# One product for the sums of keys and queries, k'v turned in one product, whole levels for two batches, and a new order of all operations

## The chip, the cores and the metric

The kernel runs on one core of a Trainium2 chip. The core has TensorE (PE: matmuls and weight loads), VectorE (DVE), ScalarE (ACT), GpSimd (POOL), SyncE (SP, which issues most transfers) and 16 DMA engines. The metric is the device time of one execution in microseconds, as the median of several runs. Times within the kernel come from one profiled execution.

## The reference, cut to what matters

The first part is a polynomial sketch attention over 4 batches, 4 heads, 1088 positions and head size 32. The second part mixes tokens with two 1088 x 1088 matrices.

```python
def phi(x):                                   # r = 8, so 64 features
    a = np.einsum('rd,bhsd->bhsr', S1, x)
    b = np.einsum('rd,bhsd->bhsr', S2, x)
    return np.einsum('bhsi,bhsj->bhsij', a, b).reshape(*x.shape[:-1], r * r)
q_p, k_p = phi(q), phi(k)
kv = np.einsum('bhsf,bhsd->bhfd', k_p, v)
z = np.sum(k_p, axis=2)
x = (q_p @ kv) / (q_p @ z + 1e-6)             # heads joined: (4, 1088, 128)
theta = x @ w_theta
zr, zi = x * np.cos(theta), x * np.sin(theta)
y = einsum('ts,bsd->btd', w_tok_r, zr) + einsum('ts,bsd->btd', w_tok_i, zi)
u = x + y
out = u + np.maximum(u @ w_ch, 0.0)
```

S1, S2 and the weights of the second part are 64-bit floats, which the kernel reads as pairs of 32-bit words and converts itself.

## The kernel before, in words

The tokens of a batch are 9 chunks of 128 (the last half empty), taken in 3 groups of 3 chunks. Heads and head size make the 128 columns.

A batch goes through these stages. `kfeatures` (741 to 774) transposes the keys, makes their features, forms outer products on DVE (761) and sums k'v on PE (770) in 32 columns of the array per head; ACT copies the sum to `kvT` (774). `key_sums` rounds the keys to a grid and forms their Gram matrix: the sum of squares of the keys comes from ACT (644 or 650), is added over the partitions by a product with ones (653) and gives the four steps `kg` (655); the Gram products (690, 703, 704 or 693) are in two halves of 64 columns; ACT copies parts of them (708, 709 or 698) for two turned products (712 or 701). `query_scale` does the same sum for the queries (937, 940) and derives their scale. `chain` (795 to 882) turns the Gram matrix into the denominators' vector for batch 0, for batch 1, and for batches 2 and 3 together: e0 and e1 on DVE and ACT (795 to 798), a first product (809), a second (847), a maximum (852), and slices `mv`, `mf`. `chain_out` turns k'v with two products, one for each half of the output's rows (901), and multiplies it by a mask (902). `query_slices` transposes and splits the queries (969 to 980). `levels` (1001) multiplies the queries by the slices, 9 products in f16 and 3 in f32 for a group, each in two halves of 64 columns of the array. DVE forms the denominators (1009 to 1030). `outputs_x` forms the outer products of the queries (1052), transposes them (on PE for batches 0 and 1, on DVE and over DRAM for 2 and 3), multiplies by k'v (1077), and then takes angle, sine and cosine (1105 to 1130).

The 17 rows of the mixing matrices are read and converted by `weight` (583 to 590): one transfer of 1.1 MB, two ACT passes, two DVE passes. `mix_row` uses a row for batch 0 in three spans of 384, 384 and 320 tokens, and for batch 1 span by span. Batches 2 and 3 share seven products in the manner of Winograd (1266), in pieces of 288 and 256 or 128 tokens. `finish` and `finish_turned` make the output.

All operations are entered by `op` with an engine and a duration. They aren't issued as they are entered: the string `ORDER` gives the numbers of all 1022 operations in the order of issue, each engine's queue being a subsequence, and `PLACES` gives the slot of each buffer in its class (8 banks of PSUM, 5 slots for raw rows, 22 large ones, and so on). An engine takes its operations strictly in that order. `SPINS` puts products on zeros (line 379, tile `idle`) ahead of certain operations of PE, which keep it busy: 10 at the start, 16 by the string, and one in the code.

Most of PE's products are issued from line 341, most of DVE's operations from lines 305, 309 and 312, so they are told apart by tile.

Of the kernel before, what the change touches and what calls it, by code (L numbers as in the profile page):

```python
# [21 lines left out]
P = 128  # L22
# [44 lines left out]
)  # L67
PLACES = (
# [8 lines left out]
)  # L77
SPINS = (
    "70:2 15:3 137:1 211:1 424:2 128:1 168:1 174:2 176:1 521:2 "
# [14 lines left out]
QGRAM = (False,) * 4  # L94
# [7 lines left out]
ADD_FLY2 = 3.1  # L102
QFIX = 2.006
# [18 lines left out]
class Layout:  # L122
# [63 lines left out]
    def issue(self, pools, fill):  # L186

        spins = dict(tuple(map(int, x.split(":"))) for x in SPINS.split())
        shared = True
        for o in self.order:  # L190
            n, home = spins.get(o.i, 0), None
            if shared:
                for _ in range(n):
                    fill()
            for b in o.bufs:
                if b.ap is None:
                    raw = pools[b.cls](b.slot)
                    home = raw if b.cls == "ps" else home
                    b.ap = view(raw, b.shape, b.dt)
            if not shared:  # L200
                for _ in range(n):
                    fill(home)
            o.fn()
            shared = shared and o is not self.parted
# [33 lines left out]
def kernel(  # L238
# [136 lines left out]
    idle = fixed((GW,), BF16, "idle")  # L375
    nowhere = buf("ps", (GW,), F32, "nowhere")

    def spin(home=None):
        T.matmul(nowhere() if home is None else view(home, (GW,), F32), idle()[:, 0:P], idle(), start=True, stop=True, skip_group_check=True)  # L379

    op("G", 0.3, lambda: G.memset(idle(), 0.0), [idle], [])  # L381
    op("P", 1.73, lambda: [spin() for _ in range(10)], [nowhere], [idle])
# [235 lines left out]
    kvb, kk, kg = {}, {}, {}  # L618

    def key_sums(b):  # L620
        at("grid", b)
        kx = ld["k", b]
        km = buf("sm", (3,), F32, "km")
        kb = buf("hf", (NC, HD), BF16, "kb")
# [7 lines left out]
        if ("k", b) in SPLIT:  # L632
# [8 lines left out]
            op("V", 0.2, lambda: V.tensor_reduce(out=km()[:, 1:2], in_=ka(), axis=AX.X, op=ALU.add), [(km, 1)], [ka])  # L641
        elif KHALF[b]:
            c = (NC + 1) // 2 * HD
            op("A", act(c) + 0.1, lambda: A.activation(flat(j_())[:, :c], kc()[:, :c], AF.Square, accum_out=km()[:, 1:2]),
               [(j_, 0), (km, 1)], [kx])
# [767 lines left out]
```

## Time and profile before

| | |
|---|---|
| median of 3 runs | 219.61 us (219.26 to 220.01) |
| span of the profiled execution, first to last instruction | 217.4 us |
| median less that span | 2.2 us |
| PE busy | 209.3 us, 1998 matmuls |
| DVE busy | 181.2 us |
| ACT busy | 111.2 us |
| POOL busy | 22.2 us |
| moved by DMA | 40.58 MB |
| mean granted clock of PE | 0.997 |

The profiled execution has no time of its own beside its span, so the span is set against the median of the runs. In a row of the timeline the first number is the start in us, the second the length; `ps<-big,zs 128*128 128x384 f32 x6` is six matmuls from tiles big and zs into PSUM, with weights of 128 rows and 128 columns and 384 streamed columns. An f32 product is two such instructions, so a mixing row of batch 0 is six. `128*64`, `128*32` and `64*64` are weights that fill a part of the array. A length includes the drain of a matmul, so neighbours overlap by some 0.15 us.

### The profile page before, as it was taken

Reading aid. Unit: us, or ns where it says so; the run is one execution under the profiler, and the core shown is the slowest. Engines: PE = TensorE matmul, PEld = TensorE weight load, DVE = VectorE, ACT = ScalarE, POOL = GpSimd, SP = SyncE. Lnnn points to the kernel's source line nnn. Section 1 sums busy time; section 2 is a strip of 40 time slices with the busy share of each in tenths; the row PEclk is TensorE's granted clock in tenths of the full one; section 3 lists DMA queues with packets and bytes.
Section 4 is the critical chain, followed back from the end, with each engine's and each line's share of the span. In section 5 each row is a group of like instructions: output and inputs, shape, how many; then the busy total and the mean of one; then the engine's idle time right before and its main releaser. Section 6 shows DMA issues by size and latency. Waiting matters only on the chain.

```text
span 217.4 us, 5063 instructions
## 1 busy us (share of the span) xinstructions
PE 209.3 (96%) x1998; PEld 154.3 (71%) x1998; DVE 181.2 (83%) x408; ACT 111.2 (51%) x214; POOL 22.2 (10%) x44
## 2 busy tenths in 40 slices
PE   7999899999999999999999999999999999999994
PEld 3987786686766686666766575667758788888883
DVE  4899999999999999999599839988138999996542
ACT  3998498899779999983322040354037400000010
POOL 2237000055000000100132000100101000000000
PEclk9999999999999999999999999999999999999998
DMA  5999996869979979894226998599911000045253
GB/s 153 429 406 340 425 399 203 333 224 271 267 276 361 361 264 380 219 198 126 33 36 102 222 137 199 105 156 151 231 78 32 0 0 0 3 66 89 36 79 75
DMA packets 52635, 40.58 MB, mean 187 GB/s; under 512 B 45444, under 2 KB 47108, under 8 KB 50436
## 3 DMA queue, kind: packets, MB, share of 16 engines
q1 hardware_dynamic: 35540, 33.71, 48.7%
q0 software_dynamic: 1728, 4.65, 10.5%
q10 hardware_dynamic: 15344, 1.90, 6.0%
q8 instruction: 15, 0.25, 0.5%
q14 instruction: 8, 0.07, 0.1%
HBM read 30.43 MB, written 5.18 MB: 164 GB/s over the span
## 4 chain that ended last, share of the span: by engine, by line
PE 72%; DVE 12%; ACT 8%; DMA 4%; ACTq 2%; issue 2%; SPq 1%
PE ps L341 66%; DMA big<-q_l 2%; DVE lv L305 2%; PE ps L1064 2%; ACTq L333 2%; PE ps L1098 1%; DMA fx<-g 1%; DVE g L305 1%; DVE big L305 1%; PE ps L967 1%; ACT big L584 1%; ACT big L937 1%; DVE hf L309 1%; DVE zs L305 1%; ACT g L1068 1%
## 5 line engine op out<-in xcount | busy, mean ns | idle before, releaser
L341 PE MATMUL ps<-big,zs 128*128 128x384 f32 (+4 forms) x398 | 109.7, 424 | 0.4 <-DVE zs L305 0.4
L341 PEld LDWEIGHTS ps<-big,zs 128*128 128x128 f32 x398 | 71.4, 190 | 30.3 <-issue 2.6
L1201 ACT COPY g<-ps 128x128 f32<-128x128 f32 (+1 forms) x3 | 0.9, 301 | 42.5 <-PE ps L1193 42.5
L305 DVE CUSTOM_DVE_ANT_0 big<-big,big 128x2176 uint16<-128x2176 uint16 x17 | 21.8, 1287 | 0.4 <-ACT big L586 0.2
L584 ACT ACTIVATE big<-zs 128x1088 f32<-128x1088 f32 x17 | 20.9, 1235 | 2.1 <-DMA zs<-w_tok 1.2
L586 ACT ACTIVATE big<-zs 128x1088 int32<-128x1088 uint32 (+1 forms) x18 | 21.3, 1184 | 0.1
L341 PE MATMUL ps<-big,big 128*64 128x64 f32 (+2 forms) x208 | 20.6, 276 | 0.0
L341 PEld LDWEIGHTS ps<-big,big 128*64 128x64 f32 (+1 forms) x208 | 16.5, 154 | 2.9 <-issue 0.2
L305 DVE TENSOR_TENSOR big<-big,big 128x544 f32<-128x544 f32 x24 | 16.7, 712 | 0.0
L1002 ACT COPY lv<-ps 128x480 f32<-128x480 f32 x12 | 6.3, 563 | 14.2 <-PE ps L341 14.2
L312 DVE SCALAR_TENSOR_TENSOR g<-g,ps 128x384 f32<-128x384 f32 x12 | 6.6, 548 | 8.1 <-ACT g L1111 8.1
L1078 ACT COPY big<-ps 128x384 f32<-128x384 f32 x12 | 5.9, 489 | 14.0 <-PE ps L341 8.3
L309 DVE TENSOR_SCALAR big<-big 128x1088 int32<-128x1088 int32 x17 | 12.2, 724 | 0.6 <-ACT big L584 0.5
L341 PEld LDWEIGHTS ps<-w,big 128*128 128x128 f32 x80 | 10.6, 192 | 2.3 <-ACT g L1068 0.6
L319 POOL DMA_DIRECT2D big<-hf x6 | 5.4, 957 | 63.3 <-DVE g L312 33.8
L319 POOL DMA_DIRECT2D g<-big x6 | 5.2, 920 | 64.8 <-ACT g L1179 34.7
L341 PE MATMUL ps<-w,big 128*128 128x128 f32 x80 | 11.8, 280 | 0.0
L305 DVE TENSOR_TENSOR g<-lv 128x768 f32<-128x768 f32 x12 | 11.2, 945 | 0.0
L341 PE MATMUL ps<-g,sm 128*64 128x384 f32 x48 | 10.1, 507 | 0.2 <-ACT big L1078 0.2
L305 DVE TENSOR_TENSOR zs<-ps,g 128x768 f32<-128x768 f32 (+2 forms) x15 | 9.4, 632 | 1.0 <-PE ps L1098 0.9
L341 PEld LDWEIGHTS <-hf 128*64 128x64 f16 (+1 forms) x288 | 7.7, 110 | 2.9 <-issue 1.7
L379 PE MATMUL ps<-idle 128*128 128x384 bf16 x27 | 7.8, 400 | 1.3 <-POOL idle L381 1.3
(194 smaller groups left out, 336.6 us busy)
## 6 DMA issues: line engine op xcount, KB each, us to landing
zs<-w_tok SPq DMA_DIRECT2D x17, 1088.0 KB, 7.0
big<-k_l SPq DMA_DIRECT2D x6, 576.0 KB, 6.6
big<-hf POOLq DMA_DIRECT2D x6, 576.0 KB, 6.0
big<-v_l SPq DMA_DIRECT2D x4, 576.0 KB, 7.0
g<-fq SPq DMA_DIRECT2D x6, 384.0 KB, 5.2
big<-q_l SPq DMA_DIRECT2D x3, 576.0 KB, 5.1
fq<-g SPq DMA_DIRECT2D x12, 96.0 KB, 4.0
fq<-g ACTq DMA_DIRECT2D x12, 96.0 KB, 4.1
```

What stands on the lines that cost most here:

```text
L305: eng.tensor_tensor(out=o, in0=a, in1=b, op=f)
L309: (eng or V).tensor_scalar(out=o, in0=a, scalar1=s1, scalar2=s2, op0=op0, **kw)
L312: (eng or V).scalar_tensor_tensor(out=o, in0=a, scalar=s, in1=b, op0=op0, op1=op1)
L319: op("G", 0.9, lambda: G.dma_start(dst(), src(), accum_op=ALU.add), w, r, fly=fly)
L333: E.dma_start(there().rearrange("(a i) (x b j) -> b i x a j", a=nf, b=nf, j=SQ)[f], blocks()[f * SQ:(f + 1) * SQ].rearrange("i (x a j) -> ...
L341: T.matmul(o, lhs, rhs, start=start, stop=stop, skip_group_check=True)
L379: T.matmul(nowhere() if home is None else view(home, (GW,), F32), idle()[:, 0:P], idle(), start=True, stop=True, skip_group_check=True)
L584: op("A", 0.22 + n * 0.0009, lambda: A.activation(dfn(), words_of(raw(), n)[1].bitcast(F32), AF.Prelu, scale=2.0**-112, alpha=-(2.0**32)), ...
L586: op("A", 0.22 + n * 0.0009, lambda: A.activation(stp(), words_of(raw(), n)[0].bitcast(U32), AF.Copy, scale=2.0**-29), [stp], [raw])
L1002: op("A", act(480), lambda g=g, lp=lp: A.copy(lv().rearrange("p l (c n) -> p l c n", n=HR)[:, :, g * GC:(g + 1) * GC], lp().rearrange("p c ...
L1064: T.transpose(tr()[:, i * P:(i + 1) * P], qp()[:, i * H + 2 * n:i * H + 2 * n + 2].rearrange("p h i j -> p (h i j)"), ident())
L1078: op("A", act(GW), lambda g=g, xp=xp: A.copy(xt()[:, g * GW:(g + 1) * GW], xp()), cells(xt, g * GW, (g + 1) * GW), [xp])
```

## The change

Sums: `key_sums` no longer has a product with ones. The sums of squares of a chain's keys and of its first query stand side by side in one buffer `kq`, and `query_scale` of the chain's first batch adds them in one product; the steps `kg` of those keys come from it. Four of eight such products go, and `kg` depends on a query's square. `query_scale` of batches 2 and 3 follows both `key_sums`.

k'v: ACT writes the copy twice side by side, and one product with 128 weight columns turns it.

Levels: for batches 0 and 1 (`LFULL`) a product has all 128 weight columns, 12 products a group in place of 24, and f32 products stand between the f16 ones, chunk by chunk.

Zeros: `idle` is f32; four 16-bit products on zeros become one f32 product of the same 384 columns. `SPINS` has 5 in place of 16.

`finish_turned` also takes widths that are multiples of 64. The unused branch `QGRAM` goes. `ORDER` and `PLACES` are new throughout, for 1018 operations.

```diff
 SPINS = (
-    "70:2 15:3 137:1 211:1 424:2 128:1 168:1 174:2 176:1 521:2 "
+    "76:2 166:2 172:1 "
 )
+LFULL = (True, True, False, False)
...
-    idle = fixed((GW,), BF16, "idle")
+    idle = fixed((GW,), F32, "idle")
...
-    op("P", 1.73, lambda: [spin() for _ in range(10)], [nowhere], [idle])
+    op("P", 1.73, lambda: [spin(None, n) for n in (4, 4, 2)], [nowhere], [idle])
...
-        kg[b] = fixed((4,), F32, f"kg{b}")
-        pg = buf("ps", (512,), F32, "pg")
-        op("P", 0.25, lambda: mm(pg()[:, 0:1], ones(), km()[:, 1:2], True, True), [pg], [(km, 1)])
-
-        vop(4, lambda: tt(V, kg[b](), steps(), pg()[:, 0:1].to_broadcast([P, 4]), ALU.mult), [kg[b]], [pg, steps])
...
-        kt = buf("sm", (R * R,), F32, "kvT")
-        op("A", act(R * R), lambda: A.copy(kt(), acc()), [kt], [acc])
+        kt = buf("sm", (2, R * R), F32, "kvT")
+        op("A", act(2 * R * R), lambda: A.copy(kt(), bc(acc(), 1, [P, 2, R * R])), [kt], [acc])
...
-            def twice(tr=tr, kt=kt):
-                for n in range(2):
-                    mm(tr()[n * R * R:(n + 1) * R * R], kt(), ident(), True, True)
-
-            op("P", 0.31, twice, [tr], [kt, mk], half=True)
+            op("P", 0.23, lambda tr=tr, kt=kt: mm(tr(), kt().rearrange("p n f -> p (n f)"), ident(), True, True), [tr], [kt, mk])
...
-        t = buf("ps", (1,), F32, "qt")
-        op("P", 0.25, lambda: mm(t(), ones(), m()[:, 0:1], True, True), [t], [m])
+        t = buf("ps", (1 + len(keys_of),), F32, "qt")
+        op("P", 0.25, lambda: mm(t(), ones(), kq(), True, True), [t], [kq])
+        for j, kb_ in enumerate(keys_of):
+            kg[kb_] = fixed((4,), F32, f"kg{kb_}")
+            col = j + (j > 0)
+            vop(4, lambda kb_=kb_, col=col: tt(V, kg[kb_](), steps(), t()[:, col:col + 1].to_broadcast([P, 4]), ALU.mult),
+                [kg[kb_]], [t, steps])
...
-            def lev(g=g, lp=lp):
+            parts = [slice(0, P)] if LFULL[b] else sides
+
+            def lev(g=g, lp=lp, sides=parts):
...
-                for i in range(GC):
                     x = f()[:, (g * GC + i) * P:(g * GC + i + 1) * P]
                     for n in sides:
-                        mm(o[n, i, 2 * HR:], x[:, n], mf[b]().rearrange("p t h r -> p (t h r)"), False, True)
-
-            op("P", 0.91, lev, [lp], [f, h, mv[b], mf[b]], half=True)
+                        mm(o[n, i, 2 * HR:], x[:, n], mf[b]().rearrange("p t h r -> p (t h r)"), False, i == GC - 1)
+
+            op("P", 1.03 if LFULL[b] else 0.91, lev, [lp], [f, h, mv[b], mf[b]], half=not LFULL[b])
...
-        n = w // P
+        n = -(-w // P)
+        m = w // n
...
-                end = finish_turned if h and not (c1 - c0) % P else finish
+                end = finish_turned if h and not (c1 - c0) % (P // 2) else finish
...
             kfeatures(b)
             key_sums(b)
+        for b in bs:
             query_scale(b)
```

Of the new order, what the prediction speaks of: SP loads query 1 ahead of query 0, w2 ahead of keys 3, values 0 and keys 2, and row 5 behind row 0. On ACT one conversion of row 0 stands ahead of batch 1's Gram copies (708, 709) and one more of row 4 ahead of chain 1's step at 798. On PE the k'v sums of batch 0 stand ahead of chain 0's second product, operations on parts of the array stand together more often, and mixing rows 6 to 11 of batch 0 come ahead of chain 2's first product. On DVE rows 5 to 11 are finished ahead of batch 1's last outer products.

More of the change, by code (lines that the diff above doesn't have):

```diff
@@ L93 @@
 KTWO = (False, False, True, True)
-QGRAM = (False,) * 4
 QDMA = (False, False, True, True)
@@ L191, in issue @@
             n, home = spins.get(o.i, 0), None
+            sizes = [4] * (n // 4) + [1] * (n % 4)
             if shared:
-                for _ in range(n):
-                    fill()
+                for x in sizes:
+                    fill(None, x)
             for b in o.bufs:
@@ L200, in issue @@
             if not shared:
-                for _ in range(n):
-                    fill(home)
+                for x in sizes:
+                    fill(home, x)
             o.fn()
@@ L373, in constants, with spin @@
         V.memset(ones(), 1.0)
-    idle = fixed((GW,), BF16, "idle")
+    idle = fixed((GW,), F32, "idle")
     nowhere = buf("ps", (GW,), F32, "nowhere")
-    def spin(home=None):
-        T.matmul(nowhere() if home is None else view(home, (GW,), F32), idle()[:, 0:P], idle(), start=True, stop=True, skip_group_check=True)
+    def spin(home=None, quarters=1):
+        o = nowhere() if home is None else view(home, (GW,), F32)
+        x = idle() if quarters > 1 else idle().bitcast(BF16)
+        w = GW * quarters // 4 if quarters > 1 else GW
+        T.matmul(o[:, :w], x[:, 0:P], x[:, :w], start=True, stop=True, skip_group_check=True)
     op("G", 0.3, lambda: G.memset(idle(), 0.0), [idle], [])
-    op("P", 1.73, lambda: [spin() for _ in range(10)], [nowhere], [idle])
+    op("P", 1.73, lambda: [spin(None, n) for n in (4, 4, 2)], [nowhere], [idle])
     op("V", 1.55, constants, [hm, bdm, halfpi, ups, steps, upv, ones], [])
@@ L615, in load @@
                                                         src[b].rearrange("p c h d -> p (c h d)")), [t], [])
-    kvb, kk, kg = {}, {}, {}
+    kvb, kk, kg, both, bothp = {}, {}, {}, {}, {}
     def key_sums(b):
@@ L623, in key_sums @@
         km = buf("sm", (3,), F32, "km")
+        first = next(bs[0] for bs in CHAINS if b in bs)
+        if b == first:
+            both[b] = buf("sm", (1 + sum(len(bs) for bs in CHAINS if b in bs),), F32, "kq")
+        kq, kc_ = both[first], (b - first) + (b > first)
         kb = buf("hf", (NC, HD), BF16, "kb")
@@ L640, in key_sums @@
                 op("A", act(n / NG) + 0.1, lambda g=g: square(g), [(j_, g), (ka, g)], [(kx, g)])
-            op("V", 0.2, lambda: V.tensor_reduce(out=km()[:, 1:2], in_=ka(), axis=AX.X, op=ALU.add), [(km, 1)], [ka])
+            op("V", 0.2, lambda: V.tensor_reduce(out=kq()[:, kc_:kc_ + 1], in_=ka(), axis=AX.X, op=ALU.add), [(kq, kc_)], [ka])
         elif KHALF[b]:
             c = (NC + 1) // 2 * HD
-            op("A", act(c) + 0.1, lambda: A.activation(flat(j_())[:, :c], kc()[:, :c], AF.Square, accum_out=km()[:, 1:2]),
-               [(j_, 0), (km, 1)], [kx])
+            op("A", act(c) + 0.1, lambda: A.activation(flat(j_())[:, :c], kc()[:, :c], AF.Square, accum_out=kq()[:, kc_:kc_ + 1]),
+               [(j_, 0), (kq, kc_)], [kx])
             op("V", dve(n - c) + 0.06, lambda: V.tensor_tensor_reduce(
                 flat(j_())[:, c:], kc()[:, c:], kc()[:, c:], 1.0, 0.0, ALU.mult, ALU.add, km()[:, 2:3]), [(j_, 1), (km, 2)], [kx], lk=1)
-            op("V", 0.16, lambda: tt(V, km()[:, 1:2], km()[:, 1:2], km()[:, 2:3], ALU.add), [(km, 1)], [(km, 2)], lk=1)
-        else:
-            op("A", act(n) + 0.1, lambda: A.activation(flat(j_()), kc(), AF.Square, accum_out=km()[:, 1:2]), [j_, (km, 1)], [kx])
-        kg[b] = fixed((4,), F32, f"kg{b}")
-        pg = buf("ps", (512,), F32, "pg")
-        op("P", 0.25, lambda: mm(pg()[:, 0:1], ones(), km()[:, 1:2], True, True), [pg], [(km, 1)])
-        vop(4, lambda: tt(V, kg[b](), steps(), pg()[:, 0:1].to_broadcast([P, 4]), ALU.mult), [kg[b]], [pg, steps])
+            op("V", 0.16, lambda: tt(V, kq()[:, kc_:kc_ + 1], kq()[:, kc_:kc_ + 1], km()[:, 2:3], ALU.add),
+               [(kq, kc_)], [(km, 2)], lk=1)
+        else:
+            op("A", act(n) + 0.1, lambda: A.activation(flat(j_()), kc(), AF.Square, accum_out=kq()[:, kc_:kc_ + 1]), [j_, (kq, kc_)], [kx])
         def key_step():
             x = km()[:, 0:1]
-            ts(x.bitcast(I32), km()[:, 1:2].bitcast(I32), 1, ALU.logical_shift_right)
+            ts(x.bitcast(I32), kq()[:, kc_:kc_ + 1].bitcast(I32), 1, ALU.logical_shift_right)
             ts(x, x, 2.0**76, ALU.mult)
-        op("V", 0.36, key_step, [(km, 0)], [(km, 1)], lk=1)
+        op("V", 0.36, key_step, [(km, 0)], [(kq, kc_)], lk=1)
         at("keys", b)
@@ L908 @@
     even = fixed((6,), F32, "even")
-    if any(QGRAM):
-        idh = fixed((HW,), F32, "idh")
-        at("tiny")
-        small(lambda: tt(G, idh(), ident()[:, 0:HW], ident()[:, HW:HD], ALU.add), [idh], [])
     def cells(x, t0, t1):
@@ L919, in query_scale @@
         x = ld["q", b]
-        m = buf("sm", (3,), F32, "qm")
+        m = buf("sm", (1,), F32, "qm")
+        mine = [bs for bs in CHAINS if bs[0] == b]
+        keys_of = list(mine[0]) if mine else []
+        kq = both[b] if mine else buf("sm", (1,), F32, "kq")
+        c = min(1, len(keys_of))
         n = NC * HD
         f = qx[b] = buf("big", (n,), F32, "qx")
-        if QGRAM[b]:
-            pq = buf("ps", (HW,), F32, "pq")
-            dg = buf("sm", (HW,), F32, "qd")
-            def gram():
-                for c in range(NC):
-                    y = x()[:, c].rearrange("p h d -> p (h d)")
-                    for n in sides:
-                        mm(pq()[n], y[:, n], y[:, n], c == 0, c == NC - 1)
-            op("P", 1.05, gram, [pq], [x], half=True)
-            op("V", 0.3, lambda: V.tensor_tensor_reduce(dg(), pq(), idh(), 1.0, 0.0, ALU.mult, ALU.add, m()[:, 0:1]),
-               [dg, m], [pq, idh])
-        else:
-            op("A", act(n) + 0.1, lambda: A.activation(f(), x().rearrange("p c h d -> p (c h d)"), AF.Square,
-                                                       accum_out=m()[:, 0:1]), [f, m], [x])
-        t = buf("ps", (1,), F32, "qt")
-        op("P", 0.25, lambda: mm(t(), ones(), m()[:, 0:1], True, True), [t], [m])
+        op("A", act(n) + 0.1, lambda: A.activation(f(), x().rearrange("p c h d -> p (c h d)"), AF.Square,
+                                                   accum_out=kq()[:, c:c + 1]), [f, (kq, c)], [x])
+        t = buf("ps", (1 + len(keys_of),), F32, "qt")
[5 more added lines that the diff above has]
+                [kg[kb_]], [t, steps])
         s = qs[b] = fixed((2,), F32, f"qs{b}")
         def scale():
-            a = m()[:, 1:2]
-            ts(a, t(), QFIX, ALU.mult, TINY, ALU.max)
+            a = m()
+            ts(a, t()[:, c:c + 1], QFIX, ALU.mult, TINY, ALU.max)
             ai = a.bitcast(I32)
@@ L950, in query_scale @@
         op("V", 0.53, scale, [m], [t])
-        op("A", 0.2, lambda: A.mul(s()[:, 0:1], m()[:, 1:2], 2.0**-49), [(s, 0)], [m])
+        op("A", 0.2, lambda: A.mul(s()[:, 0:1], m(), 2.0**-49), [(s, 0)], [m])
         small(lambda: ts(s()[:, 1:2], s()[:, 0:1], s()[:, 0:1], ALU.mult, ec()[:, 1:2], ALU.mult, eng=G), [(s, 1)],
@@ L1192, in turn @@
             for c in range(n):
-                T.transpose(ut()[:, c], u()[:, c * P:(c + 1) * P], ident())
+                T.transpose(ut()[:m, c], u()[:, c * m:(c + 1) * m], ident())
         def times():
             for c in range(n):
-                mm(po()[:, c], u()[:, c * P:(c + 1) * P], w2()[:, 1], True, True)
+                mm(po()[:m, c], u()[:, c * m:(c + 1) * m], w2()[:, 1], True, True)
         op("P", 0.11 * n, turn, [ut], keys)
         op("P", 0.22 * n, times, [po], keys + [w2])
-        op("A", act(w), lambda: A.copy(ot(), ut()), [ot], [ut])
-        vop(w, lambda: stt(ot(), po(), 0.0, ot(), ALU.max, ALU.add), [ot], [po])
-        op("S", 0.0, lambda: SY.dma_start(out[b, t0:t0 + w].rearrange("(c j) d -> j c d", j=P), ot()), [], [ot],
+        op("A", act(n * P), lambda: A.copy(ot()[:m], ut()[:m]), [ot], [ut])
+        vop(n * P, lambda: stt(ot()[:m], po()[:m], 0.0, ot()[:m], ALU.max, ALU.add), [ot], [po])
+        op("S", 0.0, lambda: SY.dma_start(out[b, t0:t0 + w].rearrange("(c j) d -> j c d", j=m), ot()[:m]), [], [ot],
            lk=1, fly=1.8, n=w)
```

88 rows, old and new, of tables (ORDER, PLACES) are left out of this document.

## The prediction

> **What bounds the kernel now.** I read the page first: the engines' shares, then the slices, then the chain that ended last.
>
> ```profile
> span 217.4 us, 5063 instructions
> PE 209.3 (96%) x1998; PEld 154.3 (71%) x1998; DVE 181.2 (83%) x408; ACT 111.2 (51%) x214; POOL 22.2 (10%) x44
> ...
> PE   7999899999999999999999999999999999999994
> ...
> DVE  4899999999999999999599839988138999996542
> ...
> PEclk9999999999999999999999999999999999999998
> DMA  5999996869979979894226998599911000045253
> GB/s 153 429 406 340 425 399 203 333 224 271 267 276 361 361 264 380 219 198 126 33 36 102 222 137 199 105 156 151 231 78 32 0 0 0 3 66 89 36 79 75
> ...
> PE 72%; DVE 12%; ACT 8%; DMA 4%; ACTq 2%; issue 2%; SPq 1%
> ```
>
> A slice is 5.4 us. PE is busy in nearly all of them at full granted clock, and 72% of the chain is PE's. But a busy PE includes matmuls on zeros (line 379), and DVE shows a 9 in slices 3 to 19, to about 103 us, as well. So two engines are full at once for the first half, and the chain in order of time is needed to tell them apart, with the sums by stretch:
>
> ```profile
> 61.04 0.88 DVE g L305
> ...
> 83.10 44.99 PE ps L341 x362
> ```
>
> ```profile
> 20.00:35.00 15.00, 13.27 (x332) 11.05 (x332) 14.79 (x40) 10.55 (x24) 0.29 (x2) 1.00 0.97 388
> ...
> 50.00:62.00 12.00, 11.82 (x107) 8.13 (x107) 11.82 (x27) 10.02 (x17) 2.09 (x3) 1.00 0.97 263
> 102.00:128.00 26.00, 26.00 (x297) 17.75 (x296) 18.95 (x36) 6.68 (x12) 4.25 (x6) 1.00 0.58 112
> ```
>
> (Columns: stretch, length, busy PE, weight loads, DVE, ACT, POOL, clock, DMA share, GB/s.) From 20 to 35 us DVE is full (14.79 of 15.00) and PE is not. From 50 to 62 us both are, and the outer products of batch 1 (the DVE piece at 61.04) stand in the chain. In 102 to 128 us DVE has 7 us to spare and PE none. I therefore sum in three parts: to 35 us by DVE, ACT and loads, 35 to 62 us by DVE or PE, whichever gains less, and after 62 us by PE.
>
> **Prices on PE.** These rows are the timeline of PE; differences of starts are used, because the length of a row includes the drain of its last matmul.
>
> ```profile
> 57.31 2.10 PE L341 MATMUL ps<-big,zs 128*128 128x384 f32 x6
> 59.34 0.34 PE L341 MATMUL ps<-ident,g 64*64 64x64 f32 x4
> ...
> 70.57 1.99 PE L341 MATMUL ps<-big,zs 128*128 128x384 f32 x6
> 72.40 0.49 PE L1098 MATMUL ps<-ident,big 128*128 128x128 f32 x3
> ```
>
> One mixing row between whole-array neighbours takes 72.40 - 70.57 = 1.83 us, and the same six matmuls between neighbours that use parts of the array (64*64, 128*64, 128*32) take 59.34 - 57.31 = 2.03 us. So a change of partition on both sides costs the neighbour 0.20 us.
>
> ```profile
> 102.10 0.57 PE L341 MATMUL ps<-mv,hf 128*64 128x96 f16 x18
> ...
> 103.02 0.55 PE L341 MATMUL ps<-mv,hf 128*64 128x96 f16 x18
> 103.40 0.68 PE L341 MATMUL ps<-mf,big 128*64 128x96 f32 x12
> 103.91 0.55 PE L341 MATMUL ps<-mv,hf 128*64 128x96 f16 x18
> ...
> 104.90 6.40 PE L341 MATMUL ps<-big,zs 128*128 128x320 f32 x20
> ```
>
> A group of levels in halves takes 103.91 - 103.02 = 0.89 us, and the last group before whole-array work takes 0.99 us, 0.10 more. A stretch of partitioned work therefore costs 0.20 + 0.10 = 0.30 us beyond its matmuls.
>
> ```profile
> 74.98 0.54 PE L341 MATMUL ps<-g,big 128*32 128x64 f32 x24
> 75.46 0.66 PE L341 MATMUL ps<-sbt,sm 64*64 64x64 f32 x16
> 76.04 0.88 PE L341 MATMUL ps<-g,big 128*32 128x64 f32 x48
> 76.85 0.94 PE L341 MATMUL ps<-w,big 128*128 128x128 f32 x6
> ```
>
> 24 matmuls of 128*32 take 0.48 us with a start and 48 take 0.81 us, so 24 alone cost 0.33 and a change of shape inside a stretch up to 0.15 us; I take 0.1, and 0 to 0.15 as bounds.
>
> **The new order.** I read off both orders by name. Operations on part of the array are the key features (64 columns), Gram products, halves of levels and numerators, k'v sums (32 columns) and the small 64*64 turns. Before, from chain 1's first product (34.9 us) to batch 1's first transposes there are 6 such stretches with 6 inner changes of shape, afterwards 3 with 5. From there to the end there were 9 with 7, and are 7 with 3. Levels of batch 1 and three turns of k'v that are now whole are counted in that. The saving is 3 x 0.30 + 1 x 0.1 = 1.0 us to 62 us, and 2 x 0.30 + 4 x 0.1 = 1.0 us after it. At 0.20 a stretch and nothing inside the two would be 0.6 and 0.4.
>
> **Levels over all columns.** Nothing in the trace has 128 weight columns in f16. The halves stream 9 f16 pairs in 103.40 - 103.02 = 0.38 us and 6 f32 pairs in 0.51 us, and streams of a whole product are no longer than those of its pair. The weight load is the question.
>
> ```profile
> 88.42 0.78 PE L341 MATMUL ps<-sm,pbd 128*128 128x128 f32 x6
> 89.03 2.05 PE L341 MATMUL ps<-big,zs 128*128 128x384 f32 x6
> ...
> 55.85 0.45 PE L341 MATMUL ps<-hf 128*64 128x64 bf16 x18
> 56.13 1.25 PE L341 MATMUL ps<-big,big 128*64 128x64 f32 x36
> ```
>
> Six f32 products with whole weights, four of them only 64 wide, take 0.61 us: 0.10 each, though streaming 64 is half of streaming 128. So f32 weights cost about 0.10 us each. In 16 bit, 18 loads of 64 columns take 0.28 us, or 0.031 per pair. Bounds for a group: 0.89 us if every load hides, 15 x 0.102 = 1.53 us if 16-bit weights cost what f32 ones do. I take 0.38 + 6 x 0.105 = 1.01, and 0.04 for the more frequent turns from f16 to f32, 1.05 us, since the 16-bit row is the nearer. That is +0.16 a group, +0.5 us for batch 1 (0 to +1.9). Batch 0's groups run at 25 to 28 us under DVE's full queue, at no cost; uncovered they add the same 0.5.
>
> The Trainium skill ("TensorE: Matmul & The Clock Gate", LDWEIGHTS (loading the stationary operand)) states that a load takes its columns divided by 1.2 in ns, whatever the contraction. For 128 columns that is 107 ns, which agrees with the 0.10 us of the f32 row; for 16 bit it would be 53 ns per 64 columns, and the trace, at 31 ns per pair, disagrees. By the page a group would be an estimated 15 x 0.107 = 1.6 us.
>
> **Turns and ones-products.**
>
> ```profile
> 55.58 0.44 PE L341 MATMUL ps<-ident,sm 128*64 128x128 f32 x4
> ...
> 90.92 0.28 PE L341 MATMUL ps<-sm,ones 128*128 128x8 f32 x2
> ```
>
> A turn of k'v in two halves takes 55.85 - 55.58 = 0.27 us; whole it is two loads, 0.21 us, so 0.06 less, 3 x after 62 us: 0.15. The doubled copy on ACT is 64 elements longer, behind which nothing waits soon: 0. Of the ones-products (0.28 us with the drain) four go, all before 35 us, where PE isn't the bound: 0. The key's step kg now also waits for the first query's square, on DVE with chain 0's e0 right behind it. But e0 also needs the turned Gram sums, whose ACT copy comes four ACT operations behind the query's square, so kg isn't last: 0, and up to 0.5 if the square is.
>
> **Zeros.** The group of zero products, and a piece of the chain:
>
> ```profile
> L379 PE MATMUL ps<-idle 128*128 128x384 bf16 x27 | 7.8, 400 | 1.3 <-POOL idle L381 1.3
> ...
> 38.51 0.33 PE ps L379 x2
> ```
>
> Of the 27 the work of 11 goes, 0.33 / 2 = 0.16 us each. After 35 us five were there and one is left: 0.65 us; the two at 38.51 stand where chain 1 is waited for, so I take 0.3 (0 to 0.65). The f32 zeros at the start stream as long in fewer instructions, and POOL's zeroing of twice the bytes is covered by the first keys' load. The other rule for turned stores changes nothing: 288 is no multiple of 64, and 256 and 128 were turned already.
>
> **To 35 us.** Here the order decides. In SP's queue query 1 is moved ahead of query 0, the weights w2 ahead of keys 3, values 0 and keys 2, and row 5 behind row 0. In ACT's queue, half of row 0's conversion now stands ahead of batch 1's Gram copy (line 708), and half of row 4's ahead of chain 1's e0 (798).
>
> ```profile
> L584 ACT ACTIVATE big<-zs 128x1088 f32<-128x1088 f32 x17 | 20.9, 1235 | 2.1 <-DMA zs<-w_tok 1.2
> ...
> 27.24 1.48 ACT L1002 COPY lv<-ps 128x480 f32<-128x480 f32 x3 [2.57 <-PE ps L341]
> ...
> 31.38 0.29 ACT L708 COPY g<-ps 128x128 f32<-128x128 f32 x1
> ...
> 34.54 0.35 ACT L798 ACTIVATE sm<-sm,kg 128x64 f32<-128x64 f32 x1 [0.91 <-DVE sm L312]
> ...
> 24.70 0.80 SPq L583 DMA_DIRECT2D zs<-w_tok  x2
> ```
>
> ACT idled 2.57 + 0.91 us there, room for the two conversions (1.235 us each). Row 0 is issued at 24.70 and its bytes come at the 400 GB/s of slices 2 to 6: with row 5 (1.1 MB) behind it and keys 3's second copy (0.6 MB) ahead, it lands 0.5 / 0.4 = 1.3 us earlier than before. The Gram copy then comes at about its 31.4 us. Chain 1 starts as before: 0. The bounds are a gain of 1.0 (DVE has a denominator step of batch 0 less ahead of e0) and a loss of 1.5 (a landing as late as if row 5 were still ahead). PE's k'v sums of batch 0 move ahead of chain 0's second product, so values 0 must have landed by then: they are the eighth load instead of the seventh, 0.26 MB or 0.6 us later, and needed earlier; I take 0 and leave it to the rival below.
>
> **The sum.** 35 to 62 us: PE gains 1.0 + 0.3 - 0.5 = 0.8; DVE has kg2, batch 1's k'v multiply and two of chain 2's e steps less ahead of batch 1's first outer product.
>
> ```profile
> 33.64 0.28 DVE L312 SCALAR_TENSOR_TENSOR sm<-ps,kg,g 128x64 f32<-128x64 f32 x1
> ```
>
> Four like this step are 1.1 us at most; the next begins before the last one's end, so I take 0.7. The lesser of the two counts, 0.7. After 62 us: 1.0 + 0.15 = 1.15. Together 1.85 us. The span would be 215.5 and, with the 2.2 us by which the median 219.61 exceeds it, the time **217.8 us**. The end of the order is as before, so its 3.4 us behind PE stays.
>
> **Rivals.**
> Row 0 comes late (the other side). Its load waits for a free buffer (SP's 24.70 follows a pause), and the buffers are assigned anew. ACT stands in order, so the Gram copy, chain 1 and all of PE's static order move with it, us for us. It must land by 30.2 (31.4 less a conversion); from 2.5 us beyond, 32.7, the kernel is slower by 0.66; one more 1.1 MB row ahead is 2.8 us and gives 220.6. For it: a DMA share of 0.97 there; against it: fewer bytes ahead. 0.27, in which I put any other in-order stall of this kind.
> 16-bit weights cost as much as f32 ones: batch 1's groups add 1.9 instead of 0.5, 219.2 us, no change. The 31 ns speaks against it. 0.05. (The Trainium skill's rule of columns over 1.2, as above, would give about the same.)
> Loads eat half: row 0 is late by 1.5 us, 219.3. 0.05.
> The forecast and what lies about it, 215.6 to 218.9: 0.63. Nearer its own bounds: 216.4 to 218.9.
>
> **The numbers.** About 0.3% (0.66 us) is what a measurement of this kernel can tell from no change. Faster 0.63, within it 0.10, slower 0.27. The range goes from all gains at their bounds without DVE's limit (to 35 us 1.0; to 62 us 0.9 + 0.15 + 0.65; after it 0.6 + 0.6 + 0.15: 4.0 less, 215.6) to the first rival with half a row more (221.0).
>
> **What would show it.** Right: the number of whole-array rows with 2.03 us falls, a level group of batch 1 takes 1.0 to 1.1 us, chain 1's first product (64*64) starts at 34 to 35.5 us, batch 3's levels end 1.5 us earlier than 128. Wrong: ACT idle on a load of w_tok before the Gram copy, a first product of chain 1 after 37 us, level groups of 1.5 us, or new PE waits for DVE between 62 and 128 us, because the mixing rows 6 to 11 are taken earlier.

## The result and the profile after

The changed kernel takes 217.0 us (median of 11 runs, 216.66 to 219.75) against 219.86 us for the kernel before beside it (11 runs, 219.26 to 221.81). The ratio is 0.988 with a 95% interval of 0.985 to 0.991, a gain of 2.6 us. Here and below, medians and ratios leave out runs more than 1.5% above the fastest of their kernel, and a ratio can differ a little from the quotient of two medians. The profiled execution took 216.8 us with a span of 215.0 us. The forecast was 217.8 us, in a range of 215.6 to 221.0.

In the changed kernel line numbers shift a little: most products are issued from line 340, zeros from 381, most DVE work from 304, 308 and 311. The page, in the same parts as before:

```profile
span 215.0 us, 4841 instructions
PE 205.4 (96%) x1877; PEld 154.8 (72%) x1877; DVE 182.6 (85%) x408; ACT 110.9 (52%) x214; POOL 22.9 (11%) x44
...
PE   7989899999999999999999999899999999999993
...
DVE  4899999999999999989899589778849999994631
...
PEclk9999999999999999999999999999999999999999
DMA  5999999999896997007633988889954201103143
...
PE 77%; DVE 11%; DMA 5%; ACT 3%; issue 2%; ACTq 0%; POOL 0%; SPq 0%; DVEq 0%; POOLq 0%
```

PE still bounds it, with 3.9 us less work and the clock at full. The PE row has a new dent in slice 26, at 134 to 140 us. Transfers are fuller up to some 64 us. The timeline of PE shows the dent (a wait for a transfer at 135.27 us) and the marks by which the forecast is judged:

```profile
23.17 0.25 PE L340 MATMUL ps<-hf 128*64 128x64 bf16 x4 [0.91 <-issue]
...
34.36 0.61 PE L340 MATMUL ps<-sbt,sm 64*64 64x64 f32 x8
...
61.09 0.82 PE L1053 MATMUL ps<-ident,g 128*128 128x128 f32 x6
...
123.38 0.32 PE L340 MATMUL ps<-mv,hf 128*64 128x96 f16 x6
...
135.27 1.51 PE L340 MATMUL ps<-g,sm 128*64 128x384 f32 x8 [1.39 <-DMA g<-fq]
...
156.20 2.16 PE L340 MATMUL ps<-g,sm 128*64 128x384 f32 x12
...
210.95 0.39 PE L340 MATMUL ps<-w,big 128*128 128x128 f32 x2
```

The same marks of the kernel before:

```profile
34.94 0.67 PE L341 MATMUL ps<-sbt,sm 64*64 64x64 f32 x8 [0.36 <-ACT sm L798]
...
62.05 1.65 PE L1064 MATMUL ps<-ident,g 128*128 128x128 f32 x12 [0.23 <-DVE g L305]
...
213.81 0.39 PE L341 MATMUL ps<-w,big 128*128 128x128 f32 x2
```

| stretch | before | after | gained | forecast |
|---|---|---|---|---|
| to chain 1's first product | 34.94 | 34.36 | 0.58 | 0 |
| from there to batch 1's first transposes | 27.11 | 26.73 | 0.38 | 0.7 |
| from there to the end of PE's last product (214.20, 211.34) | 152.15 | 150.25 | 1.90 | 1.15 |
| behind it | 3.20 | 3.66 | -0.46 | 0 |
| span | 217.4 | 215.0 | 2.4 | 1.85 |

In this pair of profiles the gain is there in all three regimes, and most of it where only PE bounds, though a wait of 1.39 us that the forecast did not have stands in that part. Each column is one execution. Over all profiles of the experiments below, the second row holds (26.67 to 26.76 us in nine profiles of the new order, 27.03 to 28.10 in five of the old), and so does the fourth (3.7 us in all nine, 3.2 in all five). The first mark scatters as widely as its gain: 34.16 to 36.50 us in the new order, 34.94 to 35.76 in the old.

### The profile page after: what moved, and what is told of

It is laid out like the page before. It is cut to its first block, busy times and chain, and to the rows that moved or that the text cites. A ratio compares the mean times of both kernels' runs of the same rounds, so it can differ in the third digit from the quotient of the medians.

```text
span 215.0 us, 4841 instructions
## 1 busy us (share of the span) xinstructions
PE 205.4 (96%) x1877; PEld 154.8 (72%) x1877; DVE 182.6 (85%) x408; ACT 110.9 (52%) x214; POOL 22.9 (11%) x44
## 4 chain that ended last, share of the span: by engine, by line
PE 77%; DVE 11%; DMA 5%; ACT 3%; issue 2%; ACTq 0%; POOL 0%; SPq 0%; DVEq 0%; POOLq 0%
PE ps L340 71%; DVE g L304 3%; DMA g<-fq 2%; DMA fq<-g 2%; PE ps L381 2%; PE ps L1087 1%; DVE lv L304 1%; DVE hf L308 1%; ACT big L920 1%; PE ps L955 1%; PE ps L1053 1%; PE ps L740 1%; DVE sm L311 1%; DMA out<-g 1%; ACT g L743 1%
## 5 line engine op out<-in xcount | busy, mean ns | idle before, releaser
L340 PE MATMUL ps<-big,big 128*64 128x64 f32 (+2 forms) x208 | 21.1, 276 | 0.4 <-DVE big L304 0.4
L304 DVE TENSOR_TENSOR big<-big,big 128x544 f32<-128x544 f32 x24 | 16.1, 712 | 0.0
L340 PE MATMUL ps<-mf,big 128*64 128x96 f32 (+1 forms) x108 | 12.7, 268 | 0.0
L340 PEld LDWEIGHTS <-hf 128*64 128x64 f16 (+2 forms) x234 | 10.3, 110 | 2.0 <-issue 1.9
L1103 ACT ACTIVATE g<-g 128x384 f32<-128x384 f32 x12 | 6.3, 522 | 9.2 <-DVE g L311 9.2
L340 PE MATMUL ps<-mv,hf 128*64 128x96 f16 (+1 forms) x162 | 10.9, 207 | 0.0
L340 PE MATMUL ps<-g,sm 128*64 128x384 f32 x48 | 9.2, 496 | 1.4 <-DMA g<-fq 1.4
```

The costliest lines, as they stand in the source:

```text
L304: eng.tensor_tensor(out=o, in0=a, in1=b, op=f)
L340: T.matmul(o, lhs, rhs, start=start, stop=stop, skip_group_check=True)
L1103: op("A", act(GW), lambda cs=cs: A.activation(cs()[:, 0], cs()[:, 1], AF.Abs), [(cs, 0)], [(cs, 1)])
```

## The experiments

Theory A was the forecast's: the gain is PE's, from fewer stretches of partitioned work, and what the whole levels cost is hidden only where DVE is full. Theory B was that the new code gains by itself (fewer products, fewer waits) and the order adds little. All times below are medians; the runs were made in three sets, each with its own runs of the kernel before (219.63, 219.54 and 219.91 us).

**The new code in the old order.** Every operation of the change was put at the place of its predecessor in the old order, with the old zeros; the sums' buffer `kq` became a fixed one, since the slots of before have no room for its life.

```diff
-            both[b] = buf("sm", (1 + sum(len(bs) for bs in CHAINS if b in bs),), F32, "kq")
+            both[b] = fixed((1 + sum(len(bs) for bs in CHAINS if b in bs),), F32, f"kq{b}")
 ORDER = ( ... the sequence of the kernel before ... )
 PLACES = ( ... its slots ... )
 SPINS = ( ... its 16 zero products ... )
```

> The code of the changed kernel (one product for the sums, k'v whole, levels of batches 0 and 1 whole and interleaved) in the order, slots and zeros of the kernel before, but for the steps kg, which stand behind the query's product. Theory A: the levels add 0.8 us for batch 1 and 0 to 0.8 for batch 0, and 0.2 for batches 2 and 3; four ones-products and the turns give back 0.3 to 0.6. So 0.4 to 1.4 us above the kernel before, 220.2 to 221.2 where it has 219.8; the whole gain of the change is then its order's. Theory B (the code gains by itself): 0.5 to 1.5 below the kernel before.

220.69 us, ratio to before 1.0065 (1.0035 to 1.0095). The code alone costs 1.06 us. The same kernel with the levels of batches 0 and 1 in halves again, all f16 products of a group ahead of its f32 ones:

```diff
-LFULL = (True, True, False, False)
+LFULL = (False, False, False, False)
...
+                for i in range(GC):
                     x = f()[:, (g * GC + i) * P:(g * GC + i + 1) * P]
```

> As the last one, with all levels in halves and sorted as in the kernel before: only the sums and k'v are changed. Theory A: 0.1 to 0.5 us below the kernel before (three turns of 0.05 and ends of stretches 0.3 each, where k'v stands at the edge of one). Theory B: the same as the one with whole levels or slower.

219.62 us, ratio 1.0004 (0.9988 to 1.002): sums in one product and k'v turned in one product give nothing that can be measured, where a tenth to half a microsecond was expected. B falls: the gain comes with the order, that is with the order, the slots and the zeros together. From the run with all the code to the changed kernel it is 1.0065 to 0.988, about 4 us. And whole levels, with the f32 products between the f16 ones in all batches, cost 1.07 us in the old order. The timelines, of one execution each, show where; the first line of each pair is chain 1's first product, the second batch 1's first transposes.

```profile
35.50 0.67 PE L341 MATMUL ps<-sbt,sm 64*64 64x64 f32 x8 [0.20 <-ACT sm L800]
...
63.60 0.63 PE L1054 MATMUL ps<-ident,g 128*128 128x128 f32 x4 [0.39 <-DVE g L305]
```

```profile
35.19 0.67 PE L341 MATMUL ps<-sbt,sm 64*64 64x64 f32 x8 [0.43 <-ACT sm L800]
...
62.43 1.66 PE L1055 MATMUL ps<-ident,g 128*128 128x128 f32 x12 [0.39 <-DVE g L305]
```

28.10 us with whole levels, 27.24 without: in the old order 0.86 us of batch 1's levels comes through.

**Halves in the new order.** The same edit in the changed kernel.

> The changed kernel and its order, with the levels of batches 0 and 1 back in halves and all f16 products of a group ahead of its f32 ones. Theory A (whole levels cost, the order gains): a group of batches 0 and 1 takes 0.89 us instead of the 1.17 seen, six groups 1.7 us less, of which batch 1's stage gives back one stretch (0.3 us); batches 2 and 3 go from 0.93 back to 0.89 a group (0.2 us). 1.0 to 1.6 us below the changed kernel, 215.4 to 216.0, if batch 0's groups are on the path, 0.6 below if not. Theory B (whole levels pay, since they take away changes of partition): 0 to 0.6 us above the changed kernel.

216.82 us, ratio 0.987 (0.985 to 0.990): 0.2 us below the changed kernel, within both intervals, and not the 0.6 or more that A had for it. Its timeline, and the sums of that stretch:

```profile
34.95 0.61 PE L340 MATMUL ps<-sbt,sm 64*64 64x64 f32 x8
...
46.42 0.76 PE L340 MATMUL ps<-mv,hf 128*64 128x96 f16 x18
...
61.62 0.82 PE L1054 MATMUL ps<-ident,g 128*128 128x128 f32 x6
```

```profile
35.00:62.00 27.00, 26.10 (x385) 19.28 (x386) 26.76 (x67) 26.10 (x50) 4.09 (x4) 1.00 0.95 315
```

PE saves 0.8 us on the levels, yet the stretch takes 26.67 us (61.62 - 34.95), as against 26.73 in the changed kernel: DVE (the third sum, 26.76 of 27.00) is full. The chains, first of the changed kernel, then with halves, show how near the two engines are:

```profile
46.11 10.94 PE ps L340 x145
```

```profile
55.66 0.88 DVE zs L304
...
56.67 0.91 PE ps L340 x6
```

With whole levels the chain is PE's from 44.47 to past 62 us; with halves it is DVE's up to 56.54, and PE waits 0.34 us for it. So in the new order the whole levels take PE just up to DVE's limit, and what halves save on PE is lost again in a wait. In the old order the same levels came through.

**Whole levels, but f16 first.** Only the second hunk of that edit.

> The changed kernel, only the f32 products of a group of levels stand behind all its f16 ones again (all batches). Theory A: an f32 product with whole weights costs its load of 0.11 us, and the first one behind f16 0.15, so a group goes from 1.17 to 9 x 0.043 + 0.15 + 5 x 0.11 = 1.09 us, and the halves of batches 2 and 3 from 0.93 to 0.89: 0.3 to 0.7 us below the changed kernel. Rival (the loads hide under neighbours in any order): no difference.

217.06 us, ratio 0.988 (0.986 to 0.991): no difference, where 0.3 to 0.7 less was expected. Batch 1's levels took 3.55 us with their entry instead of 3.80, but the stretch from chain 1's first product to batch 1's first transposes 26.68 (34.16 to 60.84) instead of 26.73.

**The price of a stretch.** Mixing rows of the changed kernel were put between partitioned work that stood together. Of PE's order, the end:

```diff
-k'v 3 (three groups), levels 3 (three groups), numerator 2_0, rows 15/0, 9/2, 8/1, 9/1, 10/1, 10/2
+k'v 3, row 15/0, k'v 3, row 9/2, k'v 3, row 8/1, levels 3, row 9/1, levels 3, row 10/1, levels 3, row 10/2, numerator 2_0
```

(Row 9/2 is row 9 for the third span of batch 1.) Rows 2/0 and 3/2 went between the groups of levels 2, row 13 of batch 0 into k'v 2, rows 11 and 12 between numerator 1_1, numerator 1_2 and chain 2.

> The changed kernel with its mixing rows (whole array, each as long as before) put between partitioned work that stood together, all of it behind 62 us: between numerator 1_1, numerator 1_2 and chain 2's products, between the groups of k'v of batch 2, of levels 2, of k'v of batch 3, of levels 3 and numerator 2_0. By the order of PE that is 11 stretches of partitioned work more and 3 changes of shape inside a stretch less; the products are the same. Theory A (a stretch costs PE 0.30 us beyond its products, an inner change 0.1): 11 x 0.30 - 3 x 0.1 = 3.0 us more than the changed kernel, 2.2 with 0.20 a stretch; rows between parts take 2.03 us or more instead of 1.83. Rival B (what changing over costs hides under the next loads, and the new order gains by shorter waits): within 0.5 us of the changed kernel.

225.49 us, ratio 1.025 (1.021 to 1.029): 8.5 us more than the changed kernel, far more than 3.0. Counted in the trace, behind batch 1's first transposes there are 18 stretches instead of 7 and 1 inner change instead of 3 (the expectation took 3 changes less, there are 2 less). The price itself is read locally. The changed kernel first, then this one:

```profile
113.44 8.87 PE L340 MATMUL ps<-big,zs 128*128 128x320 f32 x28
122.24 1.21 PE L340 MATMUL ps<-g,big 128*32 128x64 f32 x72
...
126.92 4.46 PE L340 MATMUL ps<-big,zs 128*128 128x384 f32 x14
```

```profile
126.28 0.54 PE L342 MATMUL ps<-g,big 128*32 128x64 f32 x24
126.75 0.91 PE L342 MATMUL ps<-big,zs 128*128 128x384 f32 x2
127.59 0.54 PE L342 MATMUL ps<-g,big 128*32 128x64 f32 x24
...
136.47 0.81 PE L342 MATMUL ps<-big,zs 128*128 128x320 f32 x2
```

```profile
PE ps L342 <- DMA g<-fq: 2.1, 1, 2.1
...
PE ps L342 <- DVE big L306: 0.8, 1, 0.8
```

The partitioned work took 126.92 - 122.24 = 4.68 us in one stretch; six rows at 8.80 / 14 = 0.63 us (the row of 28 products) are 3.77 us. Split they take 136.47 - 126.28 = 10.19 us, 1.74 more than the 8.45 of both; by the price, six stretches more and one inner change less are 6 x 0.30 - 0.1 = 1.7. Levels 2 gives 0.56 for two stretches, k'v 2 0.29 for one, the numerators 0.50 for two less an inner change: 3.1 us in all, 0.28 a stretch. So the price holds here. The other 4.4 us of the span aren't PE's products: waits behind 62 us, of which the two lines above are the largest, are 2.7 us more than in the changed kernel (4.04 against 1.39); the start is 0.44 us later, and 1.3 us I could not place.

**The wait at 135 us.** Rows 13/2 and 12/1 were taken ahead of numerators 2_1 and 2_2.

```diff
-numerator 2_1, numerator 2_2, row 13/2, row 12/1
+row 13/2, row 12/1, numerator 2_1, numerator 2_2
```

> The changed kernel with two mixing rows (rows 13 of piece 2 and 12 of piece 1) taken ahead of numerators 2_1 and 2_2, for whose turned queries PE waited 1.39 us at 135.27 us on a transfer through memory. Theory A (PE's order bounds the kernel there, so a stall removed is time gained): 0.8 to 1.4 us less than the changed kernel, 215.6 to 216.2 us. Rival B (what follows, turned the same way, waits as much, so the stall moves behind the numerators, to the first product of batch 2's multiplication or to batch 3's numerators): within 0.4 us.

216.63 us, ratio 0.985 (0.982 to 0.988), in a set without the changed kernel. Once more beside the changed kernel:

> The changed kernel once more, beside the next one, so that the two compare in one call: 216.5 to 217.5 us.

> The kernel with two mixing rows ahead of numerators 2_1 and 2_2 once more, beside the changed kernel. If PE's order bounds it there, 0.8 to 1.4 us less than the changed kernel, lessened by 0.4 us that a new pause between batch 3's numerators and the first multiplication costs (row of the first run): 0.4 to 1.0 less. If nothing is gained: within 0.3 us.

216.69 us for the changed kernel (ratio 0.987, 0.983 to 0.991), 216.70 us for the other (0.986, 0.983 to 0.988). The timeline of the other:

```profile
123.62 0.32 PE L342 MATMUL ps<-mv,hf 128*64 128x96 f16 x6
...
132.13 3.18 PE L342 MATMUL ps<-big,zs 128*128 128x384 f32 x10
135.24 1.51 PE L342 MATMUL ps<-g,sm 128*64 128x384 f32 x8
...
155.29 2.16 PE L342 MATMUL ps<-g,sm 128*64 128x384 f32 x12
```

The wait is gone, and from batch 3's levels to its numerators it is 31.67 us instead of 32.82 (156.20 - 123.38): 1.15 gained in that place. Of the time nothing clear is seen: side by side the two medians are the same, and 0.4 to 1.0 less was expected. The first mark alone moves by 0.8 us between profiles (34.16 to 34.95, one even at 36.50), which can hide such a gain, so it stays open whether this kernel beats the changed one. With the levels in halves as well:

> The changed kernel with the two mixing rows ahead of numerators 2_1 and 2_2, and the levels of batches 0 and 1 in halves again, the f32 products of a group behind all its f16 ones (0.89 us a group). If the stall of 1.39 us is gained whole and the levels gave 0.2 us in this order: 0.9 to 1.6 us less than the changed kernel, 215.4 to 216.1. If the stall moves on: within 0.5 us.

217.3 us, ratio 0.988 (0.985 to 0.992): nothing added, as halves give nothing in the new order.

**The zeros.** First the kernel before without the 16 that `SPINS` puts between steps (the expectation says 17; the one in the code stays).

```diff
-    "70:2 15:3 137:1 211:1 424:2 128:1 168:1 174:2 176:1 521:2 "
+    ""
```

> The kernel before without the 17 zero products that stand between its steps (the ten at the start stay). Theory A (each costs 0.16 us where PE does not wait, 5 of them behind 35 us): between 0.3 us less and 0.65 us less than before, and the granted clock stays at 1.00. Rival B (they only fill PE's waits): no change, within 0.2 us. Rival C (they keep the clock up): a granted clock below 0.97 in a slice after one of them, and more time.

220.68 us, ratio 1.005 (1.001 to 1.008), 1.1 us more than before. Its sums over short stretches:

```profile
31.00:35.00 4.00, 2.78 (x33) 1.91 (x33) 4.00 (x9) 3.09 (x9) 0.00 (x0) 1.00 0.82 298
...
36.00:37.00 1.00, 1.00 (x26) 0.77 (x16) 1.00 (x3) 1.00 (x4) 0.00 (x0) 0.50 0.50 81
...
39.00:40.00 1.00, 1.00 (x29) 0.88 (x19) 1.00 (x2) 0.56 (x3) 0.00 (x0) 0.83 0.70 153
```

The column behind POOL's is the granted clock: it halves right behind chain 1's wait, for about 3.4 us (35.9 to 39.3, an estimate from the sums over 0.2 us), and chain 1's products run at half speed. So C is right about the clock. It is so in other executions too: of the nine that the median counts, five had a mean granted clock of 0.990 to 0.992, while all 17 of the kernel before beside them had 0.997 or more. That the clock is what makes the time longer is not shown: those five took 219.62 to 221.33 us (the one in this trace 219.62, as much as the kernel before), and the four with a clock of 0.999 or 1.000 took 219.43 to 222.62.

The Trainium skill ("TensorE: Matmul & The Clock Gate", What's actually happening) says that the array's clock is gated to half after an idle window of about 3.4 us and released after a busy one. The trace agrees with the half and with 3.4 us to its release; but here PE was busy for 2.78 of the 4 us from 31 to 35, and for 3.17 of the 4 us right ahead of the fall (31.93 to 35.93), so it need not be idle for a whole window. The kernel before and the changed one without zeros, from 31 to 35 us, kept the clock at 1.00:

```profile
31.00:35.00 4.00, 3.10 (x37) 2.07 (x37) 4.00 (x9) 3.09 (x10) 0.00 (x0) 1.00 0.85 297
```

```profile
31.00:35.00 4.00, 3.35 (x58) 2.70 (x54) 4.00 (x9) 3.93 (x9) 0.00 (x0) 1.00 1.00 410
```

The second of these is the changed kernel with `SPINS` empty:

> The changed kernel without its five zero products between steps (two in the first turns, two ahead of chain 1's first product at 33.76 us, one in chain 1 at 37.39 us); the work of ten at the start and the one behind batch 0's k'v stay. Without those of the kernel before, the granted clock had fallen to 0.66 from 35 to 40 us. Theory A (the new order leaves PE fewer holes ahead of chain 1, which is why it gets by with fewer zeros, and needs none): clock 1.00 everywhere, within 0.3 us of the changed kernel. Rival B (the two ahead of chain 1 are still what holds the clock): a granted clock below 0.8 in the slices from 34 to 42 us, and 0.5 to 2 us more.

217.34 us, ratio 0.989 (0.985 to 0.993): no difference beyond the scatter. The clock in its profile is 1.00 throughout, as A has it, and B's fall is not there. A's reason, fewer holes on PE ahead of chain 1, fits these 4 us (3.35 busy), but it isn't shown to be what holds the clock: the changed kernel with halves was busy for 2.28 of the 4 us from 19.75, the one with rows between the stretches for 1.86 of the 4 us from 138.50, both at a clock of 1.00. And the kernel before without the last five alone:

```diff
-    "70:2 15:3 137:1 211:1 424:2 128:1 168:1 174:2 176:1 521:2 "
+    "70:2 15:3 137:1 211:1 424:2 128:1 168:1 "
```

> The kernel before without the five zero products behind 35 us alone (two and one in chain 1, two ahead of batch 1's levels). The forecast took 0.3 us for them (0 to 0.65). Theory A (they stand beside waits): 0 to 0.4 us less than before. Rival B (they too hold the clock): a clock below 0.9 in a slice from 38 to 50 us, and 0.3 us or more above before.

219.64 us, ratio 0.9994 (0.997 to 1.001), clock 1.00 throughout in its profile: they were worth nothing either way that these runs can tell.

## Why the prediction was right, step by step

**To 35 us (0; 0.58 gained).** The steps came as they were told. ACT and DVE in the changed kernel:

```profile
29.73 1.27 ACT L586 ACTIVATE big<-zs 128x1088 f32<-128x1088 f32 x1
31.09 0.27 ACT L709 COPY g<-ps 128x128 f32<-128x128 f32 x1
...
33.96 0.35 ACT L799 ACTIVATE sm<-sm,kg 128x64 f32<-128x64 f32 x1
```

```profile
32.67 0.28 DVE L311 SCALAR_TENSOR_TENSOR sm<-ps,kg,g 128x64 f32<-128x64 f32 x1
```

Row 0's conversion waits for no load and the Gram copy comes at 31.09 us (31.4 was forecast), so the first rival did not happen. DVE reaches its half of chain 1's e step at 32.67 us instead of 33.64, and ACT's step follows 0.58 us earlier. This is the bound that was named, a denominator step less ahead of it, and left at 0. How much of the 0.58 is the order's is open, as the mark scatters by more than that.

**35 to 62 us (0.7; 0.38 gained).** That PE and DVE both bound here was right: with halves PE saves 0.8 us and the stretch still takes 26.67. But in the changed kernel the chain is DVE's only up to 42.20 us and PE's from 44.47 on, so the 0.38 was not set by DVE's smaller gain alone, as was forecast, and the sizes were off. By PE's starts, its products gained 0.57 us where 0.8 was summed: the three groups of levels with their entry went from 2.70 to 3.79 us, 1.09 more instead of 0.5; zeros gave 0.52 instead of 0.3; the rest, fewer changes above all, 1.14 instead of 1.0. And PE's waits grew by 0.19 us, from 0.23 for DVE to 0.42 for ACT. The count was off too: in the trace there are 7 stretches with 5 inner changes before (a zero product parts two) and 3 with 4 after, 1.3 us by the price. A group of whole levels between others takes 1.17 us, not 1.05, and lies outside the 1.0 to 1.1 that was named as a sign:

```profile
46.41 0.29 PE L340 MATMUL ps<-mv,hf 128*128 128x96 f16 x3
46.54 0.43 PE L340 MATMUL ps<-mf,big 128*128 128x96 f32 x2
46.80 0.29 PE L340 MATMUL ps<-mv,hf 128*128 128x96 f16 x3
```

Three f16 products with whole weights take 46.54 - 46.41 = 0.13 us, 0.043 each, the stream that was taken for them (0.38 / 9 = 0.042). The two f32 ones take 0.26 us, 0.13 each instead of 0.105. The rival of dear 16-bit weights falls with this row; the Trainium skill's rule of columns divided by 1.2 ("TensorE: Matmul & The Clock Gate", LDWEIGHTS (loading the stationary operand)), which that section gives without regard to type, is 107 ns for 128 columns; it disagrees with 0.043 us in 16 bit and is below the 0.13 us in f32. The halves of batches 2 and 3, whose f32 products now also stand between the f16 ones, went from 0.89 to 0.93 us a group (the second of batch 2 runs from 102.98 to 103.91), which the forecast did not price.

**After 62 us (1.15; 1.90 gained).** The count of 9 stretches to 7 is what the trace shows. PE's starts, group by group, give: about 1.6 for stretches and their neighbours (1.0 was taken), 0.25 for the turns of k'v (0.15), 0.65 for three transposes and 18 Gram products that now come ahead of 62 us (not counted), 0.8 for waits of before that are gone, and -1.39 for the new wait. The price held where stretches were added, so 0.6 of the 1.6 is not explained by it. The waits of before stood in its profile and were left out of the forecast:

```profile
PE ps L341 <- DVE zs L305: 0.4, 1, 0.4
PE ps L1064 <- ACT g L1068: 0.2, 1, 0.2
PE ps L341 <- ACT big L1078: 0.2, 1, 0.2
```

The new wait comes with merging: numerators 2_1 and 2_2 stand together, so PE comes earlier to the last of three turns over memory. SP issued its read-back at 130.26 us and PE came at 133.88; before, it was issued at 131.20, with numerator 2_1 and other work between, and its numerator ran at 139.32. The chain shows it, 9.2 us of transfers:

```profile
125.88 4.32 DMA fq<-g
...
130.26 4.88 DMA g<-fq
...
135.27 1.98 PE ps L340 x9
```

The forecast looked for new waits between 62 and 128 us, and for DVE; this one came later, and for a transfer.

**Zeros (0.3).** They are 0.52 us of PE's time from 35 to 62 us, as said, but nothing of the kernel's time, by two runs. The step had no term for what zeros do for the clock; without all 16 the old order took 1.1 us more, of which the clock's part isn't known.

**Sums and turns (0 and 0.15).** Nothing that could be measured, as one run of both shows; its interval (0.9988 to 1.002) leaves room for the 0.15. (3 x 0.06 is 0.18, where the forecast wrote 0.15.)

**Around the span.** The end behind PE was to stay at "3.4 us"; it was 3.20 and grew by 0.46 us. As it did so in all nine profiles of the new order, it belongs to the change; its cause isn't known. The 2.2 us outside the span were 1.8 (216.8 - 215.0): the median had been set against the span of another run. These cancel. The upper end of the range does not follow from its words: 220.6 with one row more, and half a row (1.4 us) on top, is 222.0, not 221.0.

**How much was luck.** The mechanism of the largest part, PE's changes of mode behind 62 us, was right, and the price was confirmed. That 1.85 us came out as 2.4 is in part luck: 0.58 at the start, 0.65 for moved products, 0.8 for old waits and 0.6 more for stretches weren't in the sum, and the new wait of 1.39, the end's 0.46 and the 0.3 that the middle fell short took most of it back.

## What to carry to other kernels

Where one engine bounds, count how often its mode of work changes and price one change from neighbours in the trace (here 0.28 to 0.30 us); then look who feeds the merged work, because what was apart had time for its transfers. A cheaper instruction pays only in a stretch whose other engine isn't full, and an order can decide which: whole levels cost about 1 us in one order and nothing in another. Filler work can hold the clock, so before it is taken out as waste, look at the granted clock of several executions with and without it; how busy the engine is around it did not tell.

## What the runs showed of the hardware that was not expected

The granted clock halved at 35.9 us though PE was busy for 3.17 of the 4 us ahead, and it stayed whole where PE was busy for 1.86 and 2.28 of 4 us in other runs. So the busy share of those 4 us does not decide it. What window the chip looks at, and where its bound lies, no run here shows.

PE stops in the middle of a group of products, without a wait that the profile knows: 0.91 us at 22.27 us in the changed kernel (the row `[0.91 <-issue]` above), and between 0.8 and 2.4 us in all nine profiles of the new order, in none of five of the old order, with the code of the change or without it. From 20 to 35 us the DMA share is 1.01 to 1.02 in the new order, 0.96 to 0.99 in the old; but from 20 to 28 us it is 1.00 to 1.03 in both, so full transfers alone do not make it; that PE's instructions come late past the loads is a guess, and no run was made on it. It may be part of why the mark at 35 us varies between runs.
